# A decode attention kernel: which engine copies two of eight key blocks, and where one branch stands

## The chip, the cores and the metric

The kernel runs on one core of a Trainium2 chip. The core has five engines with instruction streams of their own: TensorE (PE, with its weight loads shown as PEld), VectorE (DVE), ScalarE (ACT), GpSimd (POOL) and SyncE (SP), which here only issues DMAs. The data memory on the core is SBUF with 128 partitions, matmul results land in PSUM, and 16 DMA engines bring the data in from HBM. The metric is the device time of the whole program in microseconds. Engines meet only through semaphores: one adds to a counter, another waits until the counter has a value.

## The reference

One query token attends over a cache of 65,536 keys and values. There are 32 query heads and 8 key and value heads, so four query heads share one key head; a head has 128 elements. All of it is bf16.

```
B, Hq, Hkv, Sq, Sk, D = 1, 32, 8, 1, 65536, 128
scores = einsum("bhqd,bhkd->bhqk", q, repeat(k, 4)) * D ** -0.5
p      = softmax(scores)
out    = einsum("bhqk,bhkd->bhqd", p, repeat(v, 4))
```

Keys and values are 268.4 MB together, and each byte is used once, for four queries.

## The kernel before

The cache is cut into units of 128 x 128 = 16,384 keys, four units for a head and 32 in all. Two units make a pair, so there are 16 pairs, two for each head; all engines but SP run a loop over heads (a *lap*), whose body holds the first and the second pair of the head, and TensorE loops over the 16 pairs. The two units of a pair are called n = 0 and n = 1.

A pair's keys and its values are 8.4 MB each. `kbuf` holds the keys of a whole pair, `bbuf` half as much, and `vbuf` the values of a whole pair. TensorE reads unit 0 from the first half of `kbuf` and unit 1 from `bbuf`. For pairs 1 to 12 (`WHOLE`) the keys arrive as one DMA into all of `kbuf` (line 416), and the second half is then copied on the core from `kbuf` to `bbuf`. For pairs 0, 13, 14 and 15 the second unit is loaded straight into `bbuf` and nothing is copied.

The copy is cut into eight blocks of 128 x 2048 bf16 (`CB` = 16 columns of keys each). Blocks 0 to 5 are copied by GpSimd (`POOL_COPIES`, line 204), which begins when VectorE has raised `pgo` (line 267); blocks 6 and 7 by ScalarE (`ACT_COPIES`, line 355), one behind its eviction 3 and one behind its eviction 7. The helper `copy_unit` (line 199) holds both: on a pair without copies it only raises the semaphores. TensorE waits for each block of `bbuf` before it transposes it (line 128), on `cpg` for GpSimd's and on `cpa` for ScalarE's.

For each unit, TensorE transposes 16 blocks of 8 x 128 keys into one of four PSUM buffers `trb` (line 131); an engine copies ("evicts") each block to `ktb` in SBUF (lines 197 and 194); TensorE then multiplies it with the queries into `qkb` (line 140), three blocks behind the transposes. ScalarE evicts every fourth block (3, 7, 11, 15), VectorE the other twelve. VectorE then takes the maximum (line 229), GpSimd spreads it over the partitions (line 390), ScalarE takes the exponentials and their sums (line 346), and TensorE multiplies with the values (line 158), 128 matmuls for a unit, whose end raises `pvd`. VectorE adds the result to `acc`.

SP issues the loads in the order K, V, K, V, and all its waits stand in that order too. It issues the keys of pair p when `kfree` says that the first unit of pair p-1 has been transposed and when `cfree` has reached 2p (line 414): two increments for each pair, one from GpSimd behind its last copy (line 388) and one from ScalarE (line 362). It issues the values of pair p when `vfree` says that the sums over the values of pair p-1 are there (raised at lines 294 and 306 on VectorE, behind its wait for `pvd`).

At the end of the second pair of each lap VectorE waits for the last sums (line 302), then branches on whether this is the last lap (line 303): on the last lap the result goes straight to the output column (line 304), otherwise `vfree` is raised and the sum is added (lines 306 to 308).

Of the kernel before, what the change touches and what calls it, by code (L numbers as in the profile page):

```python
# [6 lines left out]
AF = mybir.ActivationFunctionType  # L7
# [5 lines left out]
TB = 8  # L13
# [4 lines left out]
CB = 16  # L18
# [8 lines left out]

WHOLE = (1, 13)
POOL_COPIES = (0, 1, 2, 3, 4, 5)
ACT_COPIES = {3: (6,), 7: (7,)}  # L30

OUT_ROWS = ((16, 12), (15, 13), (14, 9, 5), (11, 10, 6, 1))

# [1 line left out]
def on_act(j):  # L35
    return j % 4 == 3


def starts(sizes):
    return [sum(sizes[:i]) for i in range(len(sizes))]  # L40


def take(e, sem, n=1):

    e.wait_ge(sem, n)
    e.sem_inc(sem, -n)  # L46


def bass_standalone__gqa_softmax__decode_kernel(nc, q, k, v, out):
    _, Hq, _, D = q.shape  # L50
    _, H, Sk, _ = k.shape
# [14 lines left out]
    def sem(name):  # L66
        return S(nc.semaphore(name))
# [37 lines left out]
    kp = [[sem(f"kp{i}_{p}") for p in range(len(K_PIECES[i]))] for i in range(2)]  # L105
    vp = [[sem(f"vp{i}_{p}") for p in range(len(V_PIECES[i]))] for i in range(2)]
    kfree, cfree, bfree = sem("kfree"), sem("cfree"), sem("bfree")
    cpg, cpa, pgo = sem("cpg"), sem("cpa"), sem("pgo")
    vfree = sem("vfree")
    trd, tra, evd, eva = sem("trd"), sem("tra"), sem("evd"), sem("eva")  # L110
    qkd, qrdy, pvd = sem("qkd"), sem("qrdy"), sem("pvd")
    cm, cma, ng, exd, sx, lrd, lra = (sem(n) for n in ("cm", "cma", "ng", "exd", "sx", "lrd", "lra"))
    acr, l_sem = sem("acr"), sem("l_sem")
    xd, xa, xg = sem("xd"), sem("xa"), sem("xg")
# [3 lines left out]
    def own(e, ins, s):  # L118
        ins.then_inc(s, 1)
        take(e, s)  # L120


    def pe_transposes(pe, n, j):
        kv = (bbuf if n else kbuf)[:, 0:T * D].rearrange("p (t d) -> p t d", d=D)
        if j * TB in starts(K_PIECES[n]):
            take(pe, kp[n][starts(K_PIECES[n]).index(j * TB)], 16)
        if n and j * TB % CB == 0:
            take(pe, cpa if j * TB // CB in sum(ACT_COPIES.values(), ()) else cpg)
        for i in range(TB):
            t = j * TB + i  # L130
            ins = pe.transpose(trb[j % NTB][:, i * P:(i + 1) * P], kv[:, t, :], ident[:, :])  # L131
        ins.then_inc(tra if on_act(j) else trd, 1)
# [55 lines left out]
    def evict(e, n, j):  # L188
        dst = ktb[:, j % NKG * TB * P:(j % NKG + 1) * TB * P]
        if on_act(j):  # L190
            take(e, tra)
            if j == G - 1:
                e.sem_inc(bfree if n else kfree, 1)
            e.activation(dst, trb[j % NTB][:, :], AF.Copy).then_inc(eva, 1)  # L194
        else:
            take(e, trd)
            e.tensor_copy(dst, trb[j % NTB][:, :]).then_inc(evd, 1)  # L197

    def copy_unit(e, lap, second, copies, op, done, x):

        def copies_now():
            for c in copies:
                off = T * D + c * CB * D
                ins = op(bbuf[:, c * CB * D:(c + 1) * CB * D], kbuf[:, off:off + CB * D])  # L204
                if c != copies[-1]:
                    ins.then_inc(done, 1)
            own(e, ins, x)
            e.sem_inc(done, 1)

        lo, hi = ((w - second + 1) // 2 for w in WHOLE)  # L210
        with e.If(lap < hi):
            if lo:
                with e.If(lap >= lo):
                    copies_now()
                with e.Else():
                    e.sem_inc(done, len(copies))
            else:
                copies_now()
        with e.Else():
            e.sem_inc(done, len(copies))  # L220

    def next_queries(e):
        own(e, e.tensor_copy(qcur[:, :], qT[:, 0:R]), xd)
        e.sem_inc(qrdy, 1)
        own(e, e.tensor_copy(qtmp[:, 0:HR - R], qT[:, R:HR]), xd)
        own(e, e.tensor_copy(qT[:, 0:HR - R], qtmp[:, 0:HR - R]), xd)

    def chunk_max(e, n):
        e.tensor_reduce(cmax[:, :], qkb[n][:, :].rearrange("p (t g) -> p g t", g=R),  # L229
                        AX.X, ALU.max).then_inc(cm, 1)  # L230

    def new_max(e, n, fresh):
        take(e, cma)
        mn, mo = m[n], m[1 - n]
        if fresh:
            e.tensor_copy(mn[:, :], cmaxa[:, :])
            e.tensor_scalar(negm[:, :], cmaxa[:, :], -scale, None, ALU.mult).then_inc(ng, 1)
        else:
            own(e, e.tensor_tensor(mn[:, :], mo[:, :], cmaxa[:, :], ALU.max), xd)  # L239
            e.tensor_tensor(dm[:, :], mo[:, :], mn[:, :], ALU.subtract)  # L240
            e.tensor_scalar(negm[:, :], mn[:, :], -scale, None, ALU.mult).then_inc(ng, 1)

    def rescale(e, n, fresh):
        take(e, sx)
        if fresh:
            own(e, e.tensor_copy(lp[:, :], rsum[:, :]), xd)
        else:
            own(e, e.tensor_tensor(acc[:, :], acc[:, :], alpha[:, :], ALU.mult), xd)  # L248
            own(e, e.tensor_tensor(lp[:, :], lp[:, :], alpha[:, :], ALU.mult), xd)
            own(e, e.tensor_tensor(lp[:, :], lp[:, :], rsum[:, :], ALU.add), xd)  # L250

    def values_done(e, n, fresh):
        e.wait_ge(pvd, 1)
        if fresh:
            own(e, e.tensor_copy(acc[:, :], pvb[n][:, 0:R]), xd)  # L255
        else:
            own(e, e.tensor_tensor(acc[:, :], acc[:, :], pvb[n][:, 0:R], ALU.add), xd)  # L257
        e.sem_inc(pvd, -1)

    def dve_pair(e, second, lap):  # L260

        fresh, last = not second, second
        for j in range(G):
            if not on_act(j):
                evict(e, 0, j)
            if j == 0:
                e.sem_inc(pgo, 1)
        for j in (0, 1, 2):
            evict(e, 1, j)
        take(e, qkd)  # L270
        chunk_max(e, 0)
        evict(e, 1, 4)
        new_max(e, 0, fresh)
        for j in (5, 6, 8, 9, 10):
            evict(e, 1, j)
        rescale(e, 0, fresh)
        if fresh:
            own(e, e.tensor_copy(otmp[:, 0:HR - R], oT[:, R:HR]), xd)
            own(e, e.tensor_copy(oT[:, 0:HR - R], otmp[:, 0:HR - R]), xd)
            e.transpose(orow[:, :], oT[:, :]).then_inc(t_o, 1)  # L280
        for j in (12, 13, 14):
            evict(e, 1, j)
        take(e, qkd)
        chunk_max(e, 1)
        new_max(e, 1, False)
        if last:
            next_queries(e)
        else:
            e.sem_inc(qrdy, 1)
        values_done(e, 0, fresh)  # L290
        rescale(e, 1, False)
        if not last:
            e.wait_ge(pvd, 1)
            e.sem_inc(vfree, 1)  # L294
            values_done(e, 1, False)
            return
        with e.If(lap == H - 1):
            e.sem_inc(acr, 1)
        e.sem_inc(lrd, 1)
        take(e, lra)  # L300
        own(e, e.reciprocal(recip[:, :], la[:, :]), xd)
        e.wait_ge(pvd, 1)
        with e.If(lap == H - 1):  # L303
            e.tensor_tensor(oT[:, HR - R:HR], pvb[1][:, 0:R], recip[:, :], ALU.mult).then_inc(t_f, 1)  # L304
        with e.Else():
            e.sem_inc(vfree, 1)
            own(e, e.tensor_tensor(acc[:, :], acc[:, :], pvb[1][:, 0:R], ALU.add), xd)
            e.tensor_tensor(oT[:, HR - R:HR], acc[:, :], recip[:, :], ALU.mult).then_inc(t_f, 1)
        e.sem_inc(pvd, -1)
# [16 lines left out]
    def vector_engine(e):  # L326
        make_identity(e)
        own(e, e.memset(oT[:, :], 0.0), xd)
        e.wait_ge(s_x, 1)
        own(e, e.tensor_copy(qT[:, :], qps[:, 0:HR]), xd)  # L330
        next_queries(e)
        with e.Fori(0, H) as lap:
            dve_pair(e, False, lap)
            dve_pair(e, True, lap)
        e.wait_ge(s_x, 2)
        e.tensor_copy(lrow[:, :], trb[0][0:R, 0:P]).then_inc(t_row, 1)  # L336
# [12 lines left out]
        e.sem_inc(exd, 1)  # L349
        e.sem_inc(sx, 1)  # L350

    def act_pair(e, second, lap):

        def copy(o, i):
            return e.activation(o, i, AF.Copy)  # L355

        for j in (3, 7, 11, 15):
            evict(e, 0, j)
            if j in ACT_COPIES:
                copy_unit(e, lap, second, ACT_COPIES[j], copy, cpa, xa)  # L360
                if j == max(ACT_COPIES):
                    e.sem_inc(cfree, 1)
        for j in (3, 7):
            evict(e, 1, j)
        exps(e, 0, not second)
        for j in (11, 15):
            evict(e, 1, j)
        exps(e, 1, False)

    def scalar_engine(e):  # L370
        e.dma_start(qsb[:, :], qf).then_inc(q_sem, 16)
        e.wait_ge(t_id, 1)
        e.activation(dscr[:, 0:1], ident[:, 0:1], AF.Exp, scale=1.0)
        e.activation(identf[:, :], ident[:, :], AF.Copy).then_inc(t_if, 1)
        with e.Fori(0, H) as lap:
            act_pair(e, False, lap)
            act_pair(e, True, lap)


    def gpsimd_engine(e):  # L380
# [105 lines left out]
```

## Time and profile before

| What | us |
|---|---|
| median of 3 runs | 629.92 |
| lowest and highest of them | 629.88, 630.03 |
| the profiled execution, whole time | 629.83 |
| its span, first to last instruction | 628.1 |
| TensorE busy | 489.8 |
| VectorE busy | 316.1 |
| ScalarE busy | 227.6 |
| GpSimd busy | 149.0 |

The profiled execution took 629.83 us, of which 1.73 us lie outside its span. All times inside the trace count from the start of the span. The profile has a page with busy times, slices of the span, DMA queues, the chain of work that ended last and the costliest groups of instructions; and views of the trace: groups of instructions by line, waits by engine, stretches of time, and a timeline. A name such as `SPq` or `DVEq` is an engine's sequencer, which handles waits, branches and semaphores. A group reads: line, engine, operation, output <- input, shapes, count, then busy time, the mean of one in ns, and the idle time in front of it.

### The profile page before, as it was taken

What the parts mean: (1) busy time and instruction counts of PE and PEld (TensorE: products, weight loads), DVE (VectorE), ACT (ScalarE), POOL (GpSimd) and SP (SyncE); (2) the same over time, 40 slices, a digit from 0 to 9 for tenths busy, and PEclk for the clock granted to TensorE, in tenths of its full rate; (3) what the DMA queues carried; (4) which work ended last, traced back from release to release, by engine and by line L of the source; (5) the groups of instructions that cost most, each with busy time, mean ns of one, the idle gap of its engine ahead of it and who ended that gap; (6) DMA issues with size and microseconds to landing.
All of it is one profiled execution on the core that took longest, in us unless ns stands there. A gap on an engine that the chain in (4) does not pass through costs nothing. (4 is left out here: it accounts for less than half of the span.)

```text
span 628.1 us, 28460 instructions
## 1 busy us (share of the span) xinstructions
PE 489.8 (78%) x12292; PEld 480.9 (77%) x12292; DVE 316.1 (50%) x698; ACT 227.6 (36%) x435; POOL 149.0 (24%) x118
## 2 busy tenths in 40 slices
PE   6751995959959598695986959779596799889896
PEld 5751995959859598695976959679596789789895
DVE  4530663817537175471744717356183565647382
ACT  2320442515425154341534416244062442414141
POOL 0000703307042070520606115060250700000000
PEclk9875886959869597795977959779596897969595
DMA  9999999999999999999999999999999999999997
GB/s 359 439 455 411 451 417 443 422 447 417 447 422 447 422 442 426 442 426 438 426 442 426 442 422 447 422 447 422 442 426 438 430 417 451 417 432 434 415 439 297
DMA packets 7635, 268.59 MB, mean 428 GB/s; under 512 B 1096, under 2 KB 1096, under 8 KB 1992
## 3 DMA queue, kind: packets, MB, share of 16 engines
q1 hardware_dynamic: 7576, 268.45, 99.3%
q8 instruction: 6, 0.10, 0.1%
q14 instruction: 5, 0.04, 0.0%
q10 hardware_dynamic: 48, 0.01, 0.0%
HBM read 268.44 MB, written 0.01 MB: 427 GB/s over the span
## 5 line engine op out<-in xcount | busy, mean ns | idle before, releaser
L197 DVE COPY ktb<-trb 128x1024 bf16<-128x1024 bf16 x384 | 254.8, 690 | 166.1 <-DVEq L46 164.3
L194 ACT ACTIVATE ktb<-trb 128x1024 bf16<-128x1024 bf16 x128 | 131.1, 1024 | 344.6 <-ACTq L46 344.6
L131 PE MATMUL trb<-ident,kbuf 128*128 128x128 bf16 x2048 | 177.2, 245 | 86.8 <-PEq L46 86.8
L131 PEld LDWEIGHTS trb<-ident,kbuf 128*128 128x128 bf16 x2048 | 144.0, 111 | 87.7 <-issue 87.7
L140 PE MATMUL qkb<-qcur,ktb 128*128 128x4 bf16 x4096 | 176.2, 165 | 13.6 <-PEq L46 12.1
L140 PEld LDWEIGHTS qkb<-qcur,ktb 128*128 128x128 bf16 x4096 | 156.4, 97 | 18.8 <-issue 16.8
L204 POOL COPY bbuf<-kbuf 128x2048 bf16<-128x2048 bf16 x72 | 132.9, 1896 | 158.3 <-POOLq L46 158.3
L131 PE MATMUL trb<-ident,bbuf 128*128 128x128 bf16 x2048 | 156.7, 219 | 4.8 <-issue 4.1
L158 PE MATMUL pvb<-pts,vbuf 128*128 128x4 bf16 x4096 | 115.1, 166 | 27.2 <-PEq L46 17.5
L158 PEld LDWEIGHTS pvb<-pts,vbuf 128*128 128x128 bf16 x4096 | 112.5, 103 | 29.4 <-issue 27.9
L131 PEld LDWEIGHTS trb<-ident,bbuf 128*128 128x128 bf16 x2048 | 117.4, 97 | 5.1 <-issue 5.1
L390 POOL PARTITION_ALL_REDUCE cmaxa<-cmax x32 | 11.9, 372 | 275.8 <-POOLq L46 275.8
L346 ACT ACTIVATE pts<-qkb,negm 128x128 bf16<-128x128 f32 x128 | 50.7, 547 | 0.0
L355 ACT ACTIVATE bbuf<-kbuf 128x2048 bf16<-128x2048 bf16 x24 | 45.7, 1902 | 0.0
L346 ACT ACTIVATION_READ_ACCUMULATOR pts<-qkb,negm 128x1 f32 x128 | 35.5, 277 | 0.0
L229 DVE TENSOR_REDUCE cmax<-qkb 128x4 f32<-128x512 f32 x32 | 22.0, 686 | 17.3 <-DVEq L46 17.3
L257 DVE TENSOR_TENSOR acc<-acc,pvb 128x4 f32<-128x4 f32 x16 | 2.5, 158 | 38.3 <-PE pvb L158 38.3
L342 ACT ACTIVATE alpha<-dm 128x4 f32<-128x4 f32 x24 | 4.9, 203 | 43.5 <-ACTq L46 43.5
L392 POOL PARTITION_ALL_REDUCE la<-lp x8 | 3.4, 431 | 37.8 <-POOLq L46 37.8
L239 DVE TENSOR_TENSOR m<-m,cmaxa 128x4 f32<-128x4 f32 x24 | 3.9, 164 | 11.7 <-DVEq L46 11.5
L248 DVE TENSOR_TENSOR acc<-acc,alpha 128x4 f32<-128x4 f32 x24 | 3.9, 164 | 11.6 <-DVEq L46 11.6
L255 DVE COPY acc<-pvb 128x4 f32<-128x4 f32 x8 | 1.3, 162 | 16.2 <-PE pvb L158 16.2
(41 smaller groups left out, 39.1 us busy)
## 6 DMA issues: line engine op xcount, KB each, us to landing
vbuf<-in_v_dram SPq DMA_DIRECT2D x5, 4096.0 KB, 30.4
bbuf<-in_k_dram SPq DMA_DIRECT2D x4, 2048.0 KB, 21.5
kbuf<-in_k_dram SPq DMA_DIRECT2D x2, 4096.0 KB, 19.9
bbuf<-in_k_dram SPq DMA_DIRECT2D x2, 4096.0 KB, 19.7
kbuf<-in_k_dram SPq DMA_DIRECT2D x2, 2048.0 KB, 18.9
kbuf<-in_k_dram SPq DMA_DIRECT2D x4, 512.0 KB, 11.9
kbuf<-in_k_dram SPq DMA_DIRECT2D x2, 1024.0 KB, 14.4
vbuf<-in_v_dram SPq DMA_DIRECT2D x1, 2048.0 KB, 30.0
```

The source lines that it names most:

```text
L131: ins = pe.transpose(trb[j % NTB][:, i * P:(i + 1) * P], kv[:, t, :], ident[:, :])
L140: ins = pe.matmul(qkb[n][:, t * R:(t + 1) * R], lhsT=ktb[:, off:off + P], rhs=qcur[:, :], start=True, stop=True)
L158: ins = pe.matmul(pvb[n][:, 0:R], lhsT=vv[:, t, :], rhs=pts[n][:, t * R:(t + 1) * R], start=t == 0, stop=t == T - 1)
L194: e.activation(dst, trb[j % NTB][:, :], AF.Copy).then_inc(eva, 1)
L197: e.tensor_copy(dst, trb[j % NTB][:, :]).then_inc(evd, 1)
L204: ins = op(bbuf[:, c * CB * D:(c + 1) * CB * D], kbuf[:, off:off + CB * D])
L229: e.tensor_reduce(cmax[:, :], qkb[n][:, :].rearrange("p (t g) -> p g t", g=R), AX.X, ALU.max).then_inc(cm, 1)
L239: own(e, e.tensor_tensor(mn[:, :], mo[:, :], cmaxa[:, :], ALU.max), xd)
L342: e.activation(alpha[:, :], dm[:, :], AF.Exp, scale=scale)
L346: ins = e.activation(pv[:, g, :], sv[:, g, :], AF.Exp, bias=negm[:, g:g + 1], scale=scale, accum_out=rsum[:, g:g + 1])
L355: return e.activation(o, i, AF.Copy)
L390: e.partition_all_reduce(cmaxa[:, :], cmax[:, :], P, bass.bass_isa.ReduceOp.max).then_inc(cma, 1)
```

## The change

Blocks 6 and 7 are copied by VectorE rather than by ScalarE. VectorE does both behind its eviction of block 0 of unit 0, waits for the second of them to end, and only then raises `cfree` and `pgo`; so GpSimd's six copies begin behind VectorE's two. ScalarE keeps only evictions and exponentials. TensorE waits for blocks 6 and 7 on `cpv` where it waited on `cpa`. VectorE's copy is a `tensor_copy` from SBUF to SBUF, with the branches of `copy_unit` on the lap around it, and these branches go from ScalarE's stream.

In the second pair of a lap, the wait for `pvd` at line 302 moves into both arms of the branch, so the branch is decided before the wait.

```diff
-ACT_COPIES = {3: (6,), 7: (7,)}
+DVE_COPIES = (6, 7)
...
         if n and j * TB % CB == 0:
-            take(pe, cpa if j * TB // CB in sum(ACT_COPIES.values(), ()) else cpg)
+            take(pe, cpv if j * TB // CB in DVE_COPIES else cpg)
...
             if j == 0:
+                copy_unit(e, lap, second, DVE_COPIES, e.tensor_copy, cpv, xd)
+                e.sem_inc(cfree, 1)
                 e.sem_inc(pgo, 1)
...
-        e.wait_ge(pvd, 1)
         with e.If(lap == H - 1):
+            e.wait_ge(pvd, 1)
             e.tensor_tensor(oT[:, HR - R:HR], pvb[1][:, 0:R], recip[:, :], ALU.mult).then_inc(t_f, 1)
         with e.Else():
+            e.wait_ge(pvd, 1)
             e.sem_inc(vfree, 1)
...
         for j in (3, 7, 11, 15):
             evict(e, 0, j)
-            if j in ACT_COPIES:
-                copy_unit(e, lap, second, ACT_COPIES[j], copy, cpa, xa)
-                if j == max(ACT_COPIES):
-                    e.sem_inc(cfree, 1)
```

More of the change, by code (lines that the diff above doesn't have):

```diff
@@ L107, in bass_standalone__gqa_softmax__decode_kernel @@
     kfree, cfree, bfree = sem("kfree"), sem("cfree"), sem("bfree")
-    cpg, cpa, pgo = sem("cpg"), sem("cpa"), sem("pgo")
+    cpg, cpv, pgo = sem("cpg"), sem("cpv"), sem("pgo")
     vfree = sem("vfree")
@@ L350, in exps, with act_pair @@
         e.sem_inc(sx, 1)
-    def act_pair(e, second, lap):
-        def copy(o, i):
-            return e.activation(o, i, AF.Copy)
+    def act_pair(e, second):
         for j in (3, 7, 11, 15):
             evict(e, 0, j)
-            if j in ACT_COPIES:
-                copy_unit(e, lap, second, ACT_COPIES[j], copy, cpa, xa)
-                if j == max(ACT_COPIES):
-                    e.sem_inc(cfree, 1)
         for j in (3, 7):
@@ L374, in scalar_engine @@
         e.activation(identf[:, :], ident[:, :], AF.Copy).then_inc(t_if, 1)
-        with e.Fori(0, H) as lap:
-            act_pair(e, False, lap)
-            act_pair(e, True, lap)
+        with e.Fori(0, H):
+            act_pair(e, False)
+            act_pair(e, True)
     def gpsimd_engine(e):
```

## The prediction

> **What bounds the kernel now.** I read the page first, for how full the DMA engines are.
>
> ```profile
> span 628.1 us, 28460 instructions
> PE 489.8 (78%) x12292; PEld 480.9 (77%) x12292; DVE 316.1 (50%) x698; ACT 227.6 (36%) x435; POOL 149.0 (24%) x118
> ...
> DMA  9999999999999999999999999999999999999997
> ...
> HBM read 268.44 MB, written 0.01 MB: 427 GB/s over the span
> ```
>
> No engine is full, but the DMA row reads 9 in all slices but the last. The next view is the one by stretches, for the middle of the run and one pair of it; the last three columns are TensorE's clock, the DMA engines' share and GB/s.
>
> ```profile
> 60.00:500.00 440.00, 345.15 (x8656) 338.82 (x8656) 223.19 (x481) 171.63 (x308) 141.81 (x99) 0.78 1.00 434
> 102.12:140.81 38.69, 30.46 (x768) 29.91 (x768) 19.18 (x40) 14.97 (x27) 11.82 (x8) 0.76 1.00 434
> ```
>
> For 440 us the DMA engines are busy all the time (share 1.00) at 434 GB/s. 268.44 MB at 434 GB/s are 618.5 us, 98% of the span. So the kernel is bound by its loads, and a change of the compute engines moves the time only in three ways: the DMA queue runs empty, the rate falls, or the piece behind the last byte changes. The first asks how early SP issues each load, so next come SP's waits and its timeline, with the landing times.
>
> ```profile
> SPq L414 <- POOLq L388: 226.1, 12, 21.8
> ...
> 96.19 0.33 SPq L437 DMA_DIRECT2D vbuf<-in_v_dram  x1
> 115.37 0.33 SPq L416 DMA_DIRECT2D kbuf<-in_k_dram  x1
> 134.76 0.33 SPq L437 DMA_DIRECT2D vbuf<-in_v_dram  x1
> ...
> vbuf<-in_v_dram SPq DMA_DIRECT2D x13, 25.5
> kbuf<-in_k_dram SPq DMA_DIRECT2D x12, 25.6
> ```
>
> A key load waits for GpSimd's last copy in 12 pairs (226.1 us in all), which looks like the bottleneck and isn't. The values issued at 96.19 land at 96.19 + 25.5 = 121.7; the next keys are issued at 115.37, 6.3 us earlier. Those keys land at 115.37 + 25.6 = 141.0; the next values are issued at 134.76, 6.2 us earlier. SP waits because it is ahead. I call these 6.3 and 6.2 us the leads: a key load that comes later by less than its lead, minus what a load needs from issue to its first data, costs nothing.
>
> What a load needs from issue to first data has no row. These bound it:
>
> ```profile
> qsb<-in_q_dram ACTq DMA_DIRECT2D x1, 8.0 KB, 3.3
> ...
> 626.91 0.25 SPq L448 DMA_DIRECT2D out_dram<-lrow  x1
> ```
>
> The 8 KB of queries land 3.3 us after issue; the 1 KB of output, issued at 626.91, has ended by the end of the span at 628.1, 1.2 us. First data comes before landing, so the start-up is at most 3.3 us, and 1.2 us is my near value, as that store too holds issue, travel and receipt. **The free delay of a key load is therefore between 6.3 - 3.3 = 3.0 and 6.3 - 1.2 = 5.1 us.** The Trainium skill, "DMA: Bandwidth & Descriptors", Specifications, gives 0.6 us to the first byte on this path, by which the free delay would be 5.7 us; no row here shows it by itself.
>
> **The change part by part.** The timeline of one pair shows how the copies lie (start, duration, engine, line):
>
> ```profile
> 103.49 0.69 DVE L197 COPY ktb<-trb 128x1024 bf16<-128x1024 bf16 x1 [6.90 <-DVEq L46]
> 103.84 11.08 POOL L204 COPY bbuf<-kbuf 128x2048 bf16<-128x2048 bf16 x6 [9.84 <-POOLq L46]
> 104.34 0.69 DVE L197 COPY ktb<-trb 128x1024 bf16<-128x1024 bf16 x1 [0.16 <-DVEq L46]
> ...
> 106.95 1.90 ACT L355 ACTIVATE bbuf<-kbuf 128x2048 bf16<-128x2048 bf16 x1
> ...
> 110.20 1.90 ACT L355 ACTIVATE bbuf<-kbuf 128x2048 bf16<-128x2048 bf16 x1
> 112.61 1.02 ACT L194 ACTIVATE ktb<-trb 128x1024 bf16<-128x1024 bf16 x1 [0.50 <-ACTq L46]
> 113.78 0.34 PE L140 MATMUL qkb<-qcur,ktb 128*128 128x4 bf16 x8 [0.56 <-PEq L46]
> ...
> 113.98 0.61 PE L131 MATMUL trb<-ident,kbuf 128*128 128x128 bf16 x8
> ...
> 114.63 0.61 PE L131 MATMUL trb<-ident,bbuf 128*128 128x128 bf16 x8
> ...
> 114.79 1.02 ACT L194 ACTIVATE ktb<-trb 128x1024 bf16<-128x1024 bf16 x1 [1.15 <-ACTq L46]
> ```
>
> *ScalarE's two copies go.* 2 x 1.90 = 3.8 us a pair. The second ends at 112.10 and delays ScalarE's eviction at 112.61, for which TensorE sat idle 0.56 us before 113.78. That stall goes. Next in line on ScalarE is only its eviction; the copies were never the last of `cfree`, which GpSimd raises at 103.84 + 11.08 = 114.92. Value on the path: nothing, TensorE is not the bound.
>
> *VectorE's two copies come.* No SBUF-to-SBUF copy of this size is on VectorE in the trace. The nearest rows, by line:
>
> ```profile
> L197 DVE COPY ktb<-trb 128x1024 bf16<-128x1024 bf16 x384 | 254.8, 690 | 166.1 <-DVEq L46 164.3 <-issue 0.4
> L204 POOL COPY bbuf<-kbuf 128x2048 bf16<-128x2048 bf16 x72 | 132.9, 1896 | 158.3 <-POOLq L46 158.3
> L355 ACT ACTIVATE bbuf<-kbuf 128x2048 bf16<-128x2048 bf16 x24 | 45.7, 1902 | 0.0
> L225 DVE COPY qtmp<-qT 128x28 bf16<-128x28 bf16 x9 | 1.6, 175 | 2.1 <-DVEq L46 2.1
> ```
>
> Low end: 0.69 us, the engine's copy of half the elements from PSUM. High end: 1.90 us, the same block on the other two engines. Between lies the engine's own line: (690 - 175)/(1024 - 28) = 0.52 ns an element, which makes 175 + 2020 x 0.52 = 1.22 us for 2048. I take 1.22, since it rests on two copies by this engine. The Trainium skill, "VectorE: DVE Perf Modes", the perf-mode tier table, says that a bf16 copy inside SBUF runs at twice the rate of one that reads PSUM, 693 ns for 2048 elements; by that the two would take 1.4 and not 2.4 us.
>
> VectorE's wait for its own copy and the branches add about 0.3 us: 0.12 for the branch (worked out below) and the 0.16 us that VectorE idles between evictions at 104.34. Together 2 x 1.22 + 0.3 = 2.7 us (bounds 1.7 and 4.1). For GpSimd the delay is larger: its begin at 103.84 lies 0.34 us before the eviction's end at 104.18, and now comes behind it, so 3.1 us (bounds 2.0 and 4.5). GpSimd then ends at 118.0 and SP issues the keys at 118.4; landing of the values at 121.7 leaves 3.3 us of lead. That covers even the worst start-up of 3.3 us just about, and the near one of 1.2 us with 2.1 us over. Cost: **nothing**. Queued behind GpSimd's copies is its spread of the maximum (next fence): it began at 118.31 after 3.39 us idle, so with copies that end at 118.0 it is not held up.
>
> *What the 2.7 us do to VectorE's queue.* Its evictions of blocks 1, 2, 4 wait behind the copies, and TensorE, with four transpose buffers, stalls for part of that. At most 2.7 us are passed on to the scores, the sums and so the next value load:
>
> ```profile
> 118.31 0.37 POOL L390 PARTITION_ALL_REDUCE cmaxa<-cmax  x1 [3.39 <-POOLq L46]
> ...
> 134.69 0.16 DVE L257 TENSOR_TENSOR acc<-acc,pvb 128x4 f32<-128x4 f32 x1 [3.00 <-PE pvb L158]
> ```
>
> The values are issued right behind those sums, at 134.76; 2.7 us later is 137.5, a lead of 3.5 us against landing at 141.0. Covered by the same bounds; the 0.56 us stall that goes gives some back. `kfree` comes with ScalarE's eviction at 114.79; 2.7 us later is 117.5, still before the copies' end. TensorE's waits for the blocks of `bbuf`: blocks 6 and 7 are now there by 107, block 5 at 118.0; TensorE begins on `bbuf` at 114.63, 0.65 us behind its group of transposes at 113.98, and each copied block is two such groups, so it wants block 5 at 114.63 + 10 x 0.65 = 121.1. Covered by 3 us.
>
> *Pairs without copies* get the branches on VectorE only, some 0.1 us; the loads of those pairs are issued from an earlier place and no copies precede them.
>
> *The branch before the wait.* In 15 pairs it makes nothing but leads longer. In the last it is on the chain that ends the program:
>
> ```profile
> 592.64 32.90 DMA vbuf<-in_v_dram
> 625.54 0.04 issue
> 625.59 0.44 PE pvb L158 x8
> 626.03 0.03 issue
> 626.05 0.05 DVEq L303
> 626.10 0.05 issue
> 626.15 0.17 DVE oT L304
> ```
>
> From the last matmul's end at 626.03 to VectorE's multiply at 626.15 are 0.12 us. Without the branch a wait takes about 0.03 us (the "issue" after the matmul). Gain: **0.09 us**, once.
>
> Sum against the profiled execution: 629.83 - 0.09 + 0 = 629.74. The profiled time is 0.09 us below the median of 629.92, so the median is forecast at 629.83. The bounds that stay inside the cover change nothing; 0.2% is 1.26 us, about what a measurement of this kernel can tell from no change.
>
> **The rivals.**
>
> *The key load comes too late (slower).* VectorE's copies cost the high end or more, GpSimd starts 4.5 us later, the keys are issued at 119.9, 1.8 us before the values land. With a start-up of 1.2 us that is still free; with 3.3 us the DMA queue is empty for 1.5 us in each pair with a key load behind copies, 12 times: +18 us, 648 us. It decides at a delay of 3.0 to 5.1 us. Against it: both unknowns must fall near their bad ends, 1.90 us is the price of engines whose copies are slower (ScalarE's eviction takes 1.02 us where VectorE's takes 0.69), and each bubble moves everything behind it later by the same amount, so nothing is regained. A mild form, 0.2 us a pair, would be 632.2.
>
> *The loads get slower or faster (either sign).* VectorE's faster reads of SBUF could disturb the DMA engines' writes, or ScalarE's absence free them. Against it: the rate is 434 GB/s over 440 us and also in this stretch, with hardly any copies of either engine:
>
> ```profile
> 20.00:60.00 40.00, 19.88 (x533) 19.27 (x530) 11.33 (x28) 7.28 (x21) 0.74 (x2) 0.68 1.02 435
> ```
>
> A change of 0.5 GB/s over the 12 pairs, as large as the rounding between 434 and 435 allows, is 0.1% of 440 us: 0.5 us, so 629.3 or 630.3, inside "the same". To pass the bound it would need 1.3 GB/s.
>
> *VectorE becomes the bound (slower).* It is busy 19.18 of 38.69 us in the pair shown; 2.4 us more make 21.6. It would need a loss of the value load's lead, 6.2 - 1.2 = 5.0 us; with the copies at 1.90 each it loses at most 4.1. At 3.3 us of start-up that would be 1.2 us a pair, 12 times, +14 us: 644. It needs the same bad ends as the first rival and comes with it.
>
> *The change doesn't give what it does (a version of the forecast).* The copies end later, not earlier, since GpSimd's six decide and now begin later; only the lead shows it.
>
> **How the numbers follow.** Forecast, hidden by the leads: 0.90. Late key or value load: 0.05, half of it mild. The rate falls by over 1.3 GB/s: 0.015; it or the loads' edges gain as much: 0.035 with anything I do not see that makes it faster. So faster 0.035, same 0.90, slower 0.065. The time is the forecast's, 629.83 rounded to 629.8. The range needs only the likeliest case: the runs before spread over 0.15 us, the rate rival at its rounding moves it by 0.5, so 629.2 to 630.4; that leaves out only what lies in the rest.
>
> **What would show it.** Right: the time between issue and landing of the key loads falls from 25.6 by 2 to 4 us, that of the value loads by less; the DMA share stays 1.00 at 434 GB/s in the middle; GpSimd's copies start 2 to 4.5 us after the first eviction's begin; ScalarE loses 24 copies and 45.7 us; the line of the branch is gone from the last chain. Wrong: key loads that land less than 20 us after issue, gaps in the DMA engines between pairs, a rate under 433, or copies on VectorE over 2 us each.

## The result, and the profile after

The changed kernel takes 636.96 us (six runs, 632.0 to 640.78), the kernel before beside it 629.94 us: a ratio of 1.0107, 95% interval 1.0087 to 1.0127. It is slower by 7 us, and its runs spread over 9 us where those of before spread over 0.15. The forecast was no change, 629.2 to 630.4.

From the page of the changed kernel (span; busy time by engine; the DMA row; bytes; the two groups of the copies), and its DMA view (count, median us from issue to landing):

```profile
span 634.9 us, 28388 instructions
PE 491.8 (77%) x12292; PEld 482.8 (76%) x12292; DVE 328.5 (52%) x722; ACT 184.5 (29%) x411; POOL 149.0 (23%) x118
...
DMA  8999999999999999999999999999999999999997
...
HBM read 268.44 MB, written 0.01 MB: 423 GB/s over the span
...
L204 POOL COPY bbuf<-kbuf 128x2048 bf16<-128x2048 bf16 x72 | 132.9, 1895 | 195.2 <-POOLq L46 195.2
...
L204 DVE COPY bbuf<-kbuf 128x2048 bf16<-128x2048 bf16 x24 | 15.4, 685 | 0.0
...
vbuf<-in_v_dram SPq DMA_DIRECT2D x13, 26.4
kbuf<-in_k_dram SPq DMA_DIRECT2D x12, 23.9
```

VectorE's copies are cheap, 0.685 us each, and the same bytes arrive at 423 and not 427 GB/s. The DMA row still reads 9. The view by stretches shows what the row hides. First the kernel before, then the changed one, around the first boundary between a value load and a key load behind copies (80 to 87 us), and over the middle; the last columns are TensorE's clock, the DMA share and GB/s:

```profile
80.00:87.00 7.00, 6.76 (x168) 6.60 (x165) 5.92 (x14) 4.20 (x12) 0.00 (x0) 1.00 1.00 431
```

```profile
80.00:87.00 7.00, 6.53 (x161) 6.24 (x157) 5.70 (x13) 4.59 (x12) 0.00 (x0) 1.00 0.95 348
60.00:500.00 440.00, 339.68 (x8501) 333.51 (x8502) 229.87 (x497) 126.71 (x282) 133.50 (x95) 0.76 1.00 428
```

At this boundary the rate is 348 GB/s and not 431, with the DMA engines "busy" 95% of the time, so their packets (the pieces in which the engines move a load) take longer. It is the costliest boundary of this run; at the next key load, from 118 to 125 us, the rate is 431 GB/s. Over the middle it is 428 and not 434 GB/s. From 60 to 500 us that is 440 x 6/434 = 6.1 us, most of the 7 us. The same pair as in the prediction, timeline of the changed kernel:

```profile
104.02 0.69 DVE L197 COPY ktb<-trb 128x1024 bf16<-128x1024 bf16 x1 [7.79 <-DVEq L46]
104.63 1.28 DVE L204 COPY bbuf<-kbuf 128x2048 bf16<-128x2048 bf16 x2
...
106.64 3.13 DVE L197 COPY ktb<-trb 128x1024 bf16<-128x1024 bf16 x5 [0.73 <-DVEq L46]
106.75 11.08 POOL L204 COPY bbuf<-kbuf 128x2048 bf16<-128x2048 bf16 x6 [12.98 <-POOLq L46]
...
118.28 0.33 SPq L412 DMA_DIRECT2D kbuf<-in_k_dram  x1
...
134.90 0.33 SPq L433 DMA_DIRECT2D vbuf<-in_v_dram  x1
```

GpSimd begins 2.73 us behind the eviction's begin and not 0.35: 1.9 us until the copies' end at 105.91, then 0.84 us of handover, in which VectorE waits for its own copy (its queue is idle 0.73 us) and raises the semaphores. The key load goes out at 118.28. The forecast for this point was 118.4. Behind this load only 0.1 us is lost; the pair shows how the delay comes about.

What became of the lead needs finer data than landing times. The trace has a record of every DMA packet. In pairs 2 to 12 a load is 128 packets of 64 KB, eight for each of the 16 DMA engines. I take as *lead* the time from a load's issue to the end of the first of the last sixteen packets of the load ahead of it: there the first DMA engine has nothing else left. The table has means over the 11 key loads and the 11 value loads, the mean duration of a load's first sixteen packets, the time of the profiled execution, from which the leads are, and the median of the runs:

```
                         key lead  first 16  value lead  first 16  profiled  median, us
before                     3.56      2.42       3.48       2.42     629.83   629.9 to 630.1
pgo behind block 1         2.73      2.43       3.44       2.42     629.95   630.01
3 copies, chained          2.70      2.43       3.90       2.42     629.64   629.53
pgo behind block 2         2.31      2.47       3.98       2.42     630.88   630.52
2 copies, chained          2.13      2.61       4.96       2.42     632.20   631.35
changed kernel             1.58      2.72       4.82       2.42     636.63   636.96
pgo behind a small copy    1.33      2.77       4.55       2.42     638.31   642.07
pgo behind block 4         0.69      2.87       4.72       2.42     640.93   641.05
vfree late                 4.20      2.43       1.48       2.82     638.69   636.94
4 copies on VectorE        2.93      2.49       2.48       2.57     633.62   634.06
```

In the kernel before a load is issued 3.56 us, not 6.3, ahead of the first idle DMA engine: the engines end a load one after the other, over 2.2 us, and the landing is seen about 0.5 us behind the last packet. (Some expectations below put this lead at 3.8 us.) The other rows are the experiments below.

The same records say where the time goes. At the 11 key loads of the changed kernel the DMA engines are idle for 2.2 us in all, as a mean of the sixteen, and their packets take 4.1 us longer than in the kernel before; together 6.3 us, of 6.8 us between the two profiled executions. For `pgo` behind block 4 it is 5.6 + 5.8 = 11.4 us, of 11.1.

### The profile page after: what moved, and what is told of

Same layout as the page of the kernel before. It is cut to its first block, busy times and chain, and to the rows that moved or that the text cites. A ratio compares the mean times of both kernels' runs of the same rounds, so it can differ in the third digit from the quotient of the medians.

```text
span 634.9 us, 28388 instructions
## 1 busy us (share of the span) xinstructions
PE 491.8 (77%) x12292; PEld 482.8 (76%) x12292; DVE 328.5 (52%) x722; ACT 184.5 (29%) x411; POOL 149.0 (23%) x118
## 5 line engine op out<-in xcount | busy, mean ns | idle before, releaser
L197 DVE COPY ktb<-trb 128x1024 bf16<-128x1024 bf16 x384 | 252.0, 690 | 163.7 <-DVEq L46 163.0
L131 PE MATMUL trb<-ident,kbuf 128*128 128x128 bf16 x2048 | 181.4, 248 | 97.4 <-PEq L46 97.3
L131 PEld LDWEIGHTS trb<-ident,kbuf 128*128 128x128 bf16 x2048 | 146.9, 112 | 98.6 <-issue 98.5
L204 DVE COPY bbuf<-kbuf 128x2048 bf16<-128x2048 bf16 x24 | 15.4, 685 | 0.0
```

## The experiments

My theory after the result, "late load": the key loads are issued too late for the DMA engines that finish first, and the first packets of such a load take longer. The rivals: VectorE's copies themselves disturb the loads or hold up the evictions; or the moved branch does it.

**Delay without the copies.** Three kernels are the kernel before with `pgo` raised later, behind VectorE's eviction of block 1, 2 or 4; a fourth adds a small copy that VectorE waits for. ScalarE copies as before. The first diff is for block 1.

```diff
-            if j == 0:
+            if j == 1:
                 e.sem_inc(pgo, 1)
```

```diff
+            if j == 2:
+                own(e, e.tensor_copy(qtmp[:, 0:HR - R], qT[:, R:HR]), xd)
                 e.sem_inc(pgo, 1)
```

> The kernel before, with one edit: VectorE raises pgo behind its eviction of block 1, not of block 0. No copy moves to VectorE. GpSimd should begin 0.85 us later, so the key loads are issued some 3.0 us before the first DMA engine has finished the values (3.8 us before the edit). Theory 'late key load': little or nothing is lost, under 0.3%, 629.9 to 631.5 us. Rivals 'VectorE's copies themselves' and 'the branch': 629.9 us, no change.

> The kernel before, with pgo raised behind VectorE's eviction of block 2. GpSimd should begin 1.7 us later, and the key loads are issued some 2.1 us before the first DMA engine runs out, about as in the changed kernel (1.3 to 2.3 us). Theory 'late key load': the same loss as the changed kernel has, 3 to 9 us, 633 to 639 us, and first packets of the key loads that take 2.5 to 3.3 us and not 2.42. Rivals 'VectorE's copies themselves' and 'the branch': 629.9 us, no change, as neither is in this kernel.

> The kernel before, with pgo raised behind VectorE's eviction of block 4. GpSimd should begin 3.4 us later, and the key loads are issued some 0.4 us before the first DMA engine runs out. Theory 'late key load': a larger loss than in the changed kernel, over 10 us, 640 to 655 us, with the DMA engines empty in between. Rivals 'VectorE's copies themselves' and 'the branch': 629.9 us, no change.

> The kernel before, without any copy on VectorE; pgo is raised behind VectorE's eviction of block 2 and a copy of 128x28 elements that VectorE waits for, so that GpSimd begins about 2.4 us later, as in the changed kernel. Theory 'late key load': between the run with 1.7 us (630.5) and the one with 3.4 us (641), at the changed kernel's own place: 634 to 640 us. Rival 'VectorE's copies themselves' make most of the loss: under 632 us.

Measured, in that order: 630.01 us (ratio 1.0001, 0.9992 to 1.0010), 630.52 (1.0007, 0.9998 to 1.0017), 641.05 (1.0180, 1.0165 to 1.0196), 642.07 (1.0205, 1.0189 to 1.0221; 638.31 to 644.67). The middle stretch, for `pgo` behind block 1, 2 and 4 and then the small copy, one fence for each kernel:

```profile
60.00:500.00 440.00, 347.49 (x8638) 341.31 (x8639) 222.38 (x480) 171.07 (x308) 140.88 (x99) 0.77 1.00 434
```

```profile
60.00:500.00 440.00, 346.68 (x8647) 340.69 (x8648) 222.38 (x480) 170.89 (x308) 139.67 (x98) 0.78 1.00 433
```

```profile
60.00:500.00 440.00, 334.98 (x8448) 328.31 (x8448) 213.71 (x470) 165.25 (x303) 132.63 (x94) 0.78 0.99 423
```

```profile
60.00:500.00 440.00, 336.95 (x8472) 330.55 (x8473) 217.87 (x483) 165.25 (x303) 132.63 (x94) 0.78 1.00 427
```

The rate falls with the delay alone, 434, 433, 423, 427 GB/s; no VectorE copy of a key block is in these kernels. So the delay by itself makes losses on both sides of the changed kernel's: 0.5 us at a mean lead of 2.31 us, with an interval that just reaches no change, and 11 to 12 us at 0.69 and 1.33. My expectation for block 2 (633 to 639 us) was too high: it started from the smallest leads of the changed kernel, and the mean lead here stayed at 2.31 us. The expectation for the small copy (634 to 640 us) was too low by 2 us; its mean lead, 1.33 us, is below the changed kernel's. Its median is above that for block 4 although its lead is longer; the lead was measured in the fastest of its four runs, 638.31 us, and by the profiled executions the order holds.

**The branch alone.** The kernel before with the second hunk of the diff and nothing else.

> The kernel before with the second edit alone: the wait for pvd moves into both arms of the branch on the lap. Theory 'late key load': nothing but the end of the program moves, 0.09 us faster, 629.85 us. Rival 'the branch': a part of the 7 us loss shows here, over 631 us.

Measured 629.86 us against 630.0, ratio 0.9998 (0.9989 to 1.0007): no difference that the runs can tell, and not a source of the loss. The chain that ends this kernel shows the step itself:

```profile
625.62 0.44 PE pvb L158 x8
626.07 0.03 issue
626.09 0.17 DVE oT L304
```

From the matmul's end to VectorE's multiply is now 0.03 us where it was 0.12.

**A late value load.** The kernel before with eight small copies, each waited for, ahead of `vfree` at both places. The key copies and their semaphores stay.

```diff
+            for _ in range(8):
+                own(e, e.tensor_copy(qtmp[:, 0:HR - R], qT[:, R:HR]), xd)
             e.sem_inc(vfree, 1)
```

> The kernel before with eight copies of 128x28 elements, each waited for, in front of each raise of vfree on VectorE (both places). The value loads go out about 2.6 us later, some 1.3 us before the first DMA engine has finished the keys. The copies of key blocks, GpSimd's begin and the key loads' conditions stay. Theory 'late key load' in its general form (a late load of any kind): 634 to 645 us. If only key loads behind copies matter: 629.9 us.

Measured 636.94 us (1.0102, 1.0088 to 1.0117). Here the key loads keep their lead (4.20 us) and the value loads have 1.48: as much loss as the changed kernel at a key lead of 1.58. The middle stretch:

```profile
60.00:500.00 440.00, 337.93 (x8471) 331.75 (x8472) 232.16 (x560) 165.06 (x303) 133.36 (x95) 0.77 1.00 425
```

So a value load that is late costs as much as a key load, with the copies and GpSimd left where they were.

**The copies on VectorE, GpSimd early.** Two tries raised `pgo` early in the changed kernel: ahead of VectorE's copies, or right behind giving the last copy to the engine, without waiting for its end. The third is the second with three blocks on VectorE (the last lines of the second diff are that kernel's alone). In the kernels the helper gets the semaphore as an argument; the second diff, and the one under "The handover by the copy's end", are shortened and write its name, `pgo`.

```diff
+                e.sem_inc(pgo, 1)
                 copy_unit(e, lap, second, DVE_COPIES, e.tensor_copy, cpv, xd)
                 e.sem_inc(cfree, 1)
-                e.sem_inc(pgo, 1)
```

```diff
-            own(e, ins, x)
+            ins.then_inc(x, 1)
+            e.sem_inc(pgo, 1)
+            take(e, x)
             e.sem_inc(done, 1)
...
-POOL_COPIES = (0, 1, 2, 3, 4, 5)
-DVE_COPIES = (6, 7)
+POOL_COPIES = (0, 1, 2, 3, 4)
+DVE_COPIES = (5, 6, 7)
```

> The changed kernel with one edit: pgo is raised ahead of VectorE's two copies, not behind them. GpSimd should begin as early as in the kernel before, and the key loads go out some 3.8 us before the first DMA engine runs out. VectorE still copies blocks 6 and 7. Theory 'late key load': the loss is gone, 629.8 us. Rival 'VectorE's copies themselves' (they disturb the loads, or hold up the evictions): the loss stays, about 637 us.

> The changed kernel with one edit: VectorE raises pgo as soon as its second copy has been given to the engine, not behind its end; cfree and the block's own semaphore still wait for the end. VectorE copies the same two blocks at the same place. GpSimd should begin some 1.25 us later than in the kernel before (2.4 us in the changed kernel), so a key load is issued about 14.5 us behind the landing of the keys before it. Theory 'late key load', whose runs without any copy on VectorE showed no loss at 14.1 us and 0.5 us at 14.9: 629.9 to 630.4 us. Rival 'VectorE's copies themselves': about 637 us.

> As the run with the early pgo, but VectorE copies blocks 5, 6 and 7 and GpSimd 0 to 4. GpSimd begins 0.65 us later than there and copies 1.9 us less, so the key loads go out as early as in the kernel before; the evictions and so the value loads wait for 0.65 us more. Theory 'late load' (of keys or values): 629.8 to 630.5 us. Rival 'VectorE's copies themselves': over 637 us. If the key load's lead alone counted, it would not be slower than the kernel before.

All three expectations failed: 655.43 us (1.0399, 1.0384 to 1.0414), 656.62 (1.0416, 1.0395 to 1.0438) and 662.37 (1.0515, 1.0501 to 1.0528). They don't test what they were meant to, since they bring a new cost. The copies of the first of them, by line (duration in ns: min, median, max) and in the timeline:

```profile
L204 POOL COPY bbuf<-kbuf x72: 1887/1889/2360, 65.1 to 524.3; 128x2048 bf16<-128x2048 bf16 x72
L204 DVE COPY bbuf<-kbuf x24: 2107/2274/2377, 65.4 to 516.5; 128x2048 bf16<-128x2048 bf16 x24
...
104.53 0.69 DVE L197 COPY ktb<-trb 128x1024 bf16<-128x1024 bf16 x1 [3.16 <-DVEq L46]
104.88 11.99 POOL L204 COPY bbuf<-kbuf 128x2048 bf16<-128x2048 bf16 x6 [5.95 <-POOLq L46]
105.14 4.47 DVE L204 COPY bbuf<-kbuf 128x2048 bf16<-128x2048 bf16 x2
...
110.24 1.89 DVE L197 COPY ktb<-trb 128x1024 bf16<-128x1024 bf16 x3 [0.63 <-DVEq L46]
```

VectorE's copy takes 2.27 us beside GpSimd's and 0.685 alone; the next eviction, at 110.24, starts 5.7 us behind the first one's begin at 104.53 (2.6 us in the changed kernel: 106.64 and 104.02), and both kinds of load are late (mean leads of 0.31 us for keys and 1.33 us for values). The Trainium skill, "SBUF — State Buffer", Who interferes with whom, says that a VectorE instruction that uses both port pairs and a GpSimd instruction exclude each other for a whole instruction; the trace fits that, as each copy grew by 1.59 us, near one GpSimd copy of 1.89. In the second kernel VectorE's copies start at 104.60 and GpSimd's at 104.57: the raise behind the queued copy took effect before the copies had even begun, so here a raise that isn't tied to the copy's end orders nothing.

**More copies on VectorE.** The changed kernel with blocks 4 to 7 on VectorE and 0 to 3 on GpSimd.

> The changed kernel, but VectorE copies blocks 4 to 7 and GpSimd 0 to 3. GpSimd begins another 1.3 us later and has 3.8 us less to copy, so the key loads go out about 2.5 us earlier than in the changed kernel, as early as before. Theory 'late key load': 629.8 us, the loss gone although VectorE copies twice as much. Rival 'VectorE's copies themselves': the loss doubles, about 644 us.

Measured 634.06 us (1.0065, 1.0052 to 1.0078): less than the changed kernel's loss, but not none, so neither number came. Its key lead is 2.93 us in the mean, from 0.54 to 4.68; its value lead fell to 2.48. VectorE now holds its evictions back by 2.5 us of copies, and TensorE stalls. In some pairs TensorE's clock stays low after that. Two pairs of this kernel, each from just behind its first eviction's begin, with the clock in the third column from the right:

```profile
104.00:113.00 9.00, 7.82 (x156) 7.58 (x155) 7.67 (x13) 2.05 (x2) 5.50 (x3) 0.82 0.98 422
144.00:155.00 11.00, 9.82 (x138) 9.58 (x137) 7.57 (x12) 2.05 (x2) 7.32 (x4) 0.50 0.96 417
```

At a granted clock of 0.50 fewer matmuls get done in more time. In the pair at 144 us GpSimd's copies end at 155.08, but the key load goes out at 158.43: it waits for the transposes, not for the copies. By the packet records the late key loads cost 1.9 us in all and the late value loads 2.3, against 3.8 us between the profiled executions. How much of that comes from the clock and how much from the copies' delay is not shown.

**The handover by the copy's end.** The clean test: the last copy's own completion raises `pgo`; GpSimd, having seen it, raises `cpv` for that block and `cfree` for VectorE. The engines' copies don't overlap, and VectorE doesn't wait; GpSimd begins 0.46 us behind the end of the last copy, where it was 0.84.

```diff
-            own(e, ins, x)
-            e.sem_inc(done, 1)
+            ins.then_inc(pgo, 1)
...
                     take(e, pgo)
+                    e.sem_inc(cpv, 1)
+                    e.sem_inc(cfree, 1)
```

> The changed kernel, but VectorE doesn't wait for its second copy: the end of that copy itself raises pgo, and GpSimd, once it has seen it, raises the semaphore of block 7 and cfree for VectorE. Copies of the two engines still never overlap. GpSimd should begin 1.6 us later than in the kernel before (2.4 us in the changed kernel); the key loads are issued about 14.9 us behind the landing of the keys before, as in the run with pgo behind block 2 (630.5 us). Theory 'late load': 630.0 to 631.5 us. Rival 'VectorE's copies themselves disturb the loads': about 637 us still.

> As the run with pgo raised by the copy's own end, but VectorE copies blocks 5, 6 and 7 and GpSimd 0 to 4. GpSimd begins 0.65 us later than there and has 1.9 us less to do, so the key loads go out 13.6 us behind the landing, nearly as early as in the kernel before (13.25). Theory 'late load': 629.8 to 630.2 us, no loss left although VectorE makes three copies a pair. Rival 'VectorE's copies themselves': 637 us or more.

Measured 631.35 us with two copies on VectorE (1.0025, 1.0014 to 1.0035) and 629.53 with three (0.9992, 0.9983 to 1.0000). Of the second, the copies and the middle stretch:

```profile
104.36 1.89 DVE L204 COPY bbuf<-kbuf 128x2048 bf16<-128x2048 bf16 x3
106.17 3.13 DVE L197 COPY ktb<-trb 128x1024 bf16<-128x1024 bf16 x5
106.72 9.24 POOL L204 COPY bbuf<-kbuf 128x2048 bf16<-128x2048 bf16 x5 [12.69 <-POOLq L46]
...
60.00:500.00 440.00, 344.40 (x8633) 339.73 (x8634) 240.13 (x515) 128.35 (x284) 118.70 (x87) 0.76 1.00 434
```

With three copies a pair on VectorE the rate is 434 GB/s again and nothing is lost. GpSimd begins just as late as in the changed kernel (106.72 and 106.75) but ends 1.9 us earlier, at 115.96 where it was 117.83. So VectorE's copies are not the cause; what counts is when GpSimd's work ends. This version is the fastest run here, 0.46 us under the kernel before; the interval touches 1, so I claim no more than that it isn't slower.

## Why the prediction was wrong

*That the loads bind and that only three things can move the time* held. Two of them moved, both at the boundary of two loads: the rate fell, and to a smaller part the queue ran empty.

*The delay of the key load* held in sum, not in its terms. VectorE's copy was put at 1.22 us and took 0.685, the low end of the bounds. The tier table of the Trainium skill's "VectorE: DVE Perf Modes" has 693 ns, and the trace agrees. The handover was put at 0.3 us and took 0.84. GpSimd began 2.4 us later (2.73 - 0.35) against a forecast of 3.1, and the key load of the pair shown went out at 118.28 against 118.4. That it lies so near is partly luck: the first eviction of this pair came 0.53 us later than in the kernel before, and against that eviction the key load went out 2.4 us later, not 3.0.

*The free delay of a key load, "between 3.0 and 5.1 us", is the step that failed.* The term that was mis-sized is the lead. It was counted to the landing of the load ahead, 6.3 us, but the DMA engines finish one after the other: the first has nothing left 3.56 us after the issue. The bounds of the other term, the start-up of 1.2 to 3.3 us, hold as a size: a mean lead of 2.7 us cost nothing, 2.3 us cost 0.5 us in all, 1.6 us cost 7. Its picture was too simple, though. The first packets of a late load begin 0.94 us after the issue at the earliest (`pgo` behind block 4). But data that begin in time are not enough: behind block 2 hardly any DMA engine is idle, and the first packets already take 2.47 us where 2.42 is usual. With the right lead the same sum gives 3.56 - 3.3 = 0.3 to 3.56 - 1.2 = 2.4 us. Measured, a delay of 3.56 - 2.73 = 0.8 us was free and one of 3.56 - 2.31 = 1.3 us was not quite; the change asked for 2.4.

*The rival "the key load comes too late"* named this mechanism, with a chance of 0.05. Its point of decision, a delay of 3.0 to 5.1 us, was the wrong one for the reason above. Its picture of an empty queue is a part of what came: of the 6.3 us that the packet records show, 2.2 are idle DMA engines and 4.1 are packets that take longer (2.72 us in the mean for the first sixteen, where 2.42 is usual). Its mild form, 0.2 us a pair, is small against the 0.6 us (7/12) measured.

*The value loads* were to come up to 2.7 us later; in the pair shown they went out at 134.90 where it was 134.76, and their mean lead rose to 4.82 us, as the loads ahead of them end later. *ScalarE's relief* is near the forecast: it is busy 184.5 us where it was 227.6, 24 copies less, worth nothing. *The branch* gives its 0.09 us on the last chain, too little to measure.

*The signs named.* A rate under 433, named as a sign of being wrong, is what came (428). That the time between issue and landing of the key loads falls from 25.6 us by 2 to 4 was put down as a sign of being right; it fell by 1.7, to 23.9, because late loads also take longer to arrive. Such a fall shows only that the delay came, not that it was free.

## What to carry to other kernels

In a kernel bound by its loads, a wait of the DMA queue with a comfortable lead may have little to give: measure the lead to the first DMA engine that runs out, not to the landing, and find the lead that is needed by delaying a semaphore in small steps. Work moved from a parallel engine to one that stands ahead of another adds its whole time and the handover to the chain, even if the work itself is faster; here it helped to let the end of the work raise the semaphore (636.96 to 631.35 us) and then to shorten what stands behind (629.53). A busy share of 1.00 does not say that the rate is whole.

## What the runs showed of the hardware

A load that is issued late is slow at its start: its first packets of 64 KB take 2.7 to 2.9 us in the mean instead of 2.42 us, and at the costliest boundary of the changed kernel the rate is 348 GB/s instead of 431. It holds for key loads and value loads alike. The DMA engines are idle for less time than the packets are longer, 0.2 us a boundary in the changed kernel. Why the first packets are slow stays open: no view of the trace shows it, and no run was made for it.

The time goes up steeply below a mean lead of about 2.3 us, and the runs scatter with it (630.25 to 633.52 us at a mean lead of 2.13, 632.0 to 640.78 at 1.58). My reading, which no run shows by itself, is that each late boundary shifts the next pair's work and so its lead.

VectorE's 128x2048 copy inside SBUF takes 0.685 us alone and 2.27 us, in the median, beside GpSimd's copies.
